# A convolution's output, transposed by DMA instead of by the matrix engine

## The chip, the cores and the metric

The kernel runs on one core of a Trainium2 chip. The core has five engines that each follow their own list of instructions: TensorE (PE, matrix products), VectorE (DVE), ScalarE (ACT), GpSimd (POOL) and SyncE (SP). POOL and SP issue most DMAs. The metric is the device time of one execution in microseconds (us), lower is better.

## What is computed

```python
# x: (8, 4160, 192), weight: (8 heads, 7 taps)
w = softmax(weight, axis=-1)
x_pad = concat([zeros((B, 6, D)), x], axis=1)
# each head owns 24 of the 192 channels; causal convolution over 7 rows
y = einsum('hk,bskhg->bshg', w, unfold(x_pad)).reshape(B, S, D)

# channel mix on y; y_prev is y moved by one row, with a zero row first
xk = mu_k * y + (1 - mu_k) * y_prev
xr = mu_r * y + (1 - mu_r) * y_prev
k  = maximum(xk @ w_k, 0)            # w_k: (192, 1024)
v  = (k * k) @ w_v                   # w_v: (1024, 192)
r  = sigmoid(xr @ w_r)               # w_r: (192, 192)
out = r * v
```

## The kernel before

**Pairs, groups, steps, slots.** The eight sequences are worked on in four pairs. A pair has two sides to its work. The convolution makes its rows in blocks of 116 rows, nine blocks to a group, four groups to a pair (pair 0 splits its first group into five and four blocks). The channel mix takes rows in steps of 512 rows of both sequences, eight steps and a tail of 64 rows. A slot is one of the eight 128-wide pieces of the 1024 hidden units of one step, so a pair has 65 slots, the last of them for the tail, and the whole run 260. Slots are run two at a time ("a pair of slots").

**Convolution.** `load_x` (L70) brings a group of x into `xb` by a casting DMA on POOL's queue, one DMA for each sequence (two for a sequence's first block); `xb` has three buffers. The taps, after the softmax on DVE and ACT (L121 to L130), are written into `w_row`, stored to DRAM (`w_scr`, L137) and read back with a shifted pattern as banded matrices, `toe` (L139). `conv_mm` (L183) is one matmul per head and group, with `toe` as weights; `conv_out` (L197) copies its result from PSUM to `y`, on ACT (in the first group every second one on DVE). `y` has rows on partitions; it has two buffers.

**Transposes.** The mix needs channels on partitions. `tr_mm` (L213) transposes two blocks at a time on PE, three transposes of 128 channels for each block, into PSUM; `tr_out` (L228) copies them on DVE into `yT`, whose three planes are channels 0 to 127 of each sequence, and the last 64 channels of both.

**Mix.** `diff` (L243) subtracts the neighbouring row in `yT`, `mix` (L256) forms `xk` and `xr` on DVE. `k_mm` (L297) makes one slot of k: two matmuls with 128 rows of weights and two with 64, the latter in two halves of the array's rows. `k_relu` (ACT) and `k_square` (DVE) follow. `r_mm`, `r_sig` (ACT), `v_mm` (eight matmuls) and `v_out` (DVE) make the output, two slots at a time, which SP stores from `o_sb` (four buffers).

**Order.** All engines' instructions are issued in the order of a table written out by hand: `at(table, slot, function, ...)` puts a call into a slot for one engine, and the loop at L477 walks the slots from -60. Within a slot POOL's early loads come first, then `k_mm`, then the entries for ACT, PE and DVE. Group g of pair p that is first needed in slot n0 has its conv matmuls in slots c0 to c0 + 7, with c0 = n0 - 22, its transposes from r0 = n0 - 13 on, `diff` in slot n0 - 7 and its x loads in slot c0 - 14. The second and third group of pair 0 are put later (c0 = n0 - 15, r0 = n0 - 7). `r_mm` runs 8 slots behind `k_mm`, `v_mm` 10. PSUM tiles of conv, transposes and r share a pool of two buffers (`psM`).

**The start.** The x load of the first group goes out first, then the weights' loads: `load_w(wk)` (L177) in the program's text, `load_rest` (L168: `wr`, `wv` and zeroed tiles) in slot -16. `nc.scalar.preload_act_table(AF.Sigmoid)` at L147 stands behind the softmax in the text.

Of the kernel before, what the change touches and what calls it, by code (L numbers as in the profile page):

```python
# [7 lines left out]
FP32 = mybir.dt.float32  # L8
BF16 = mybir.dt.bfloat16
AF = mybir.ActivationFunctionType  # L10
# [4 lines left out]
def kernel(  # L15
# [11 lines left out]
    nc = tc.nc  # L27

    B, S, D = x.shape
    H, K = weight.shape  # L30
    G = D // H
    DF = moe_w_k.shape[1]
    P = 128
    NF = DF // P
    LO = D - P
    HALO = K - 1
    BLK = 116
    GB = 9
    NG = 4
    STEP = 512  # L40
    NSTEP = S // STEP
    TAIL = S - NSTEP * STEP
    NPAIR = B // 2
    SPP = NSTEP * NF + 1
    NSLOT = NPAIR * SPP
    YC = 2
    LAG_V = NF + 2
    LAG_R = NF

    const = ctx.enter_context(tc.tile_pool(name="const", bufs=1))  # L50
    two = ctx.enter_context(tc.tile_pool(name="two", bufs=2))
# [4 lines left out]
    psM = ctx.enter_context(tc.tile_pool(name="psM", bufs=2, space=bass.MemoryType.PSUM))  # L56
    dram = ctx.enter_context(tc.tile_pool(name="dram", bufs=1, space=bass.MemoryType.DRAM))


    groups = [  # L60
        [(g * GB, GB, 2 * g) for g in range(NG)]
        if p
        else [(0, 5, 0), (5, 4, 1)] + [(g * GB, GB, 2 * g) for g in range(1, NG)]
        for p in range(NPAIR)
    ]

# [3 lines left out]
    def load_x(p, g):  # L70
        blk0, nb, _ = groups[p][g]
        xb = three.tile([P, GB, 2, D], BF16, tag="xb", name="xb")
        xbs[p, g] = xb
        for s in range(2):
            b = 2 * p + s
            lo, hi = 0, nb
            if blk0 == 0:
                lo = 1
                nc.gpsimd.memset(xb[0:32, 0, s, :], 0.0)
                nc.gpsimd.dma_start(out=xb[HALO:P, 0, s, :], in_=x[b, 0 : P - HALO, :])  # L80
            t0 = blk0 * BLK - HALO
            if b == B - 1 and blk0 + nb == NG * GB:
                hi = nb - 1
                r0 = t0 + hi * BLK
                nc.gpsimd.memset(xb[96:P, hi, s, :], 0.0)
                nc.gpsimd.dma_start(out=xb[0 : S - r0, hi, s, :], in_=x[b, r0:S, :])
            nc.gpsimd.dma_start(  # L87
                out=xb[:, lo:hi, s, :],
                in_=bass.AP(
                    tensor=x.tensor,  # L90
                    offset=x.offset + (b * S + t0 + lo * BLK) * D,
                    ap=[[D, P], [BLK * D, hi - lo], [1, D]],
                ),
            )
# [4 lines left out]
        out=w_raw,  # L99
        in_=bass.AP(tensor=weight.tensor, offset=weight.offset, ap=[[0, P], [K, H], [1, K]]),  # L100
    )
    nc.scalar.preload_act_table(AF.Exp)
    ones_t = const.tile([P, P], BF16)
# [3 lines left out]
    w_row = const.tile([P, H, P], BF16)  # L107
    nc.vector.memset(w_row, 0.0)
    load_x(0, 0)
    ident = const.tile([P, P], BF16)  # L110
    nc.gpsimd.affine_select(
        out=ident,
        in_=ones_t,
# [3 lines left out]
        base=0,  # L117
        channel_multiplier=-1,
    )
    w_max = const.tile([P, H], FP32)  # L120
    nc.vector.tensor_reduce(out=w_max, in_=w_raw, axis=mybir.AxisListType.X, op=ALU.max)  # L121
    w_exp = const.tile([P, H, K], FP32)
    nc.vector.tensor_tensor(
        out=w_exp, in0=w_raw, in1=w_max.unsqueeze(2).to_broadcast([P, H, K]), op=ALU.subtract
    )
    nc.scalar.activation(out=w_exp, in_=w_exp, func=AF.Exp)
    w_sum = const.tile([P, H], FP32)
    nc.vector.tensor_reduce(out=w_sum, in_=w_exp, axis=mybir.AxisListType.X, op=ALU.add)
    nc.vector.reciprocal(out=w_sum, in_=w_sum)
    nc.vector.tensor_tensor(  # L130
        out=w_row[:, :, 0:K],
# [5 lines left out]
    nc.sync.dma_start(out=w_scr, in_=w_row)  # L137
    toe = const.tile([P, H, BLK], BF16)
    nc.sync.dma_start(  # L139
        out=toe,  # L140
        in_=bass.AP(
            tensor=w_scr.tensor,
            offset=w_scr.offset + K - 1,
            ap=[[H * P - 1, P], [P, H], [1, BLK]],
        ),
    )
    nc.scalar.preload_act_table(AF.Sigmoid)  # L147


    mu = const.tile([P, 2, 2], FP32)  # L150
# [12 lines left out]
    def load_w(w, src):  # L163
        nc.gpsimd.dma_start(out=w[:, 0, :], in_=src[0:P, :])
        nc.gpsimd.dma_start(out=w[0:LO, 1, :], in_=src[P:D, :])
        nc.gpsimd.dma_start(out=w[LO:P, 1, :], in_=src[P:D, :])

    def load_rest():  # L168
# [5 lines left out]
        for t in tails:  # L174
            nc.gpsimd.memset(t, 0.0)

    load_w(wk, moe_w_k)  # L177


    ys, yTs = {}, {}  # L180
    conv_ps = {}

    def conv_mm(p, g, h):  # L183
        nb = groups[p][g][1]
        if h == 0:
            ys[p, g] = two.tile([P, GB, 2 * D], BF16, tag="y", name="y")
        ps = psM.tile([P, GB, 2, G], FP32, tag="m", name="ps_c")
        conv_ps[p, g, h] = ps
# [19 lines left out]
            n = c1 - max(c0, P)  # L208
            copy(out=yl[:, :, :, c1 - P - n : c1 - P], in_=ps[:BLK, :nb, :, G - n : G])

    tr_ps = {}

    def tr_mm(p, g, j):  # L213
        blk0, nb, _ = groups[p][g]
        if blk0 == 0 and j == 0:
            yTs[p] = two.tile([P, 3, YC + NG * GB * BLK], BF16, tag="yT", name="yT")
            nc.vector.memset(yTs[p][:, :, 0:YC], 0.0)
        ps = psM.tile([P, 3, 2, BLK], BF16, tag="m", name="ps_t")
        tr_ps[p, g, j] = ps
        for i in range(min(2, nb - 2 * j)):  # L220
            for c in range(3):
                nc.tensor.transpose(  # L222
                    out=ps[:, c, i, :],
                    in_=ys[p, g][:BLK, 2 * j + i, c * P : (c + 1) * P],
                    identity=ident[:BLK, :BLK],
                )

    def tr_out(p, g, j):  # L228
        blk0, nb, _ = groups[p][g]
        ps = tr_ps.pop((p, g, j))  # L230
        n = min(2, nb - 2 * j)
        c0 = YC + (blk0 + 2 * j) * BLK
        nc.vector.tensor_copy(  # L233
# [6 lines left out]
    def step_len(s):  # L240
        return STEP if s < NSTEP else TAIL

    def diff(p, s):  # L243
        L = step_len(s)
        c0 = YC + s * STEP
        d = two.tile([P, 3, STEP], BF16, tag="diff", name="d")
# [9 lines left out]
    def mix(p, s, i, part):  # L256

        L = step_len(s)
        c0 = YC + s * STEP - 1
        d, yT = diffs[p, s], yTs[p]  # L260
# [32 lines left out]
    def where(n):  # L293
        p, r = divmod(n, SPP)
        return p, r // NF, r % NF
# [131 lines left out]
    early, pe, act, dve = ({} for _ in range(4))  # L427

    def at(table, n, fn, *a):
        table.setdefault(n, []).append((fn, a))  # L430

    at(early, -16, load_rest)
    for p in range(NPAIR):
        for g, (blk0, nb, s0) in enumerate(groups[p]):
            n0 = p * SPP + s0 * NF
            late = p == 0 and s0 in (1, 2)
            c0, r0 = (n0 - 15, n0 - 7) if late else (n0 - 22, n0 - 13)
            if n0:
                at(early, c0 - 14, load_x, p, g)
            for h in range(H):  # L440
                at(pe, c0 + h, conv_mm, p, g, h)
                if n0 == 0 and h % 2:
                    at(dve, c0 + 1 + h, conv_out, p, g, h, nc.vector.tensor_copy)
                else:
                    at(act, c0 + 1 + h, conv_out, p, g, h, nc.scalar.copy)
            for j in range((nb + 1) // 2):
                at(pe, r0 + j, tr_mm, p, g, j)
                at(dve, r0 + 1 + j, tr_out, p, g, j)
        for s in range(NSTEP + 1):
            n0 = p * SPP + s * NF  # L450
            late = p == 0 and s in (1, 2)
            at(dve, n0 - (4 if late else 7), diff, p, s)
            for j, (i, part) in enumerate(((0, 0), (0, 1), (1, 0), (1, 1))):
                at(dve, n0 + ((-3, -2, -1, -1)[j] if late else j - 5), mix, p, s, i, part)
    for m in range(NSLOT):
        p, s, t = where(m)
        at(pe, m + LAG_R, r_mm, m)
        last = t % 2 == 1 or s == NSTEP
        if last:
            q = m - t % 2  # L460
            at(act, m + LAG_R + 1, r_sig, q)
            at(dve, m + LAG_V + 1, v_out, q)
        at(pe, m + LAG_V, v_mm, m)

# [4 lines left out]
    def slots():  # L469

        n = -60
        while n < NSLOT + LAG_V + 3:
            two_ = 0 <= n < NSLOT and where(n)[1] < NSTEP
# [48 lines left out]
```

## Time and profile before

| | |
|---|---|
| median of 3 runs | 504.35 us (503.9 to 504.45) |
| profiled execution | 503.97 us, span of its instructions 502.3 us |
| TensorE (PE) busy | 459.3 us, 91% |
| VectorE (DVE) busy | 420.6 us, 84% |
| ScalarE (ACT) busy | 375.6 us, 75% |
| GpSimd (POOL) busy | 45.9 us, 9% |
| DMA | 41.92 MB written by the queues, q0 (POOL) 26.6% and q1 (SP) 17.2% of 16 engines' span |

Busy time is the union of an engine's instructions. PE's matmuls are pipelined, so a matmul's own duration (0.25 us for 192 columns) is longer than the time after which the next one starts; starts are the better measure. "idle before <-X" says what ended an engine's wait. Times in the timeline are from the start of the span.

### The profile page before, as it was taken

The page shows a single profiled execution, that of the slowest core. Times are in us where ns is not written, and L with a number is a line of the kernel's source. Part 1 is how long each engine was busy: PE and PEld are TensorE (multiplying, and loading weights), DVE is VectorE, ACT ScalarE, POOL GpSimd, SP SyncE. Part 2 cuts the span into 40 slices and gives each one's busy share as a digit, 9 for nine tenths or more (in the row PEclk, how much of TensorE's full clock was granted, in tenths as well). Part 3 has the DMA queues.
Part 4 walks back from the last instruction along what each step waited for, and adds up shares of the span by engine and source line. Part 5 has one row for each costly group of instructions (what it writes and reads, how often), then busy time and mean ns, then how long its engine had stood idle before and what let it go on. Part 6 is the DMA issues. An engine that isn't in the chain of part 4 may idle for free.

```text
span 502.3 us, 10506 instructions
## 1 busy us (share of the span) xinstructions
PE 459.3 (91%) x4193; PEld 312.9 (62%) x4256; DVE 420.6 (84%) x676; ACT 375.6 (75%) x545; POOL 45.9 (9%) x69
## 2 busy tenths in 40 slices
PE   0587999999999999999999999999999999999996
PEld 0334666666776666666776666666676666666676
DVE  1487897989889898898899889798998989799872
ACT  3288769687786968778686877868787786967772
POOL 7512100101020010101002010100200000000000
PEclk9999999999999999999999999999999999999999
DMA  9996361826336182722718272351811212112113
GB/s 125 139 141 88 58 117 56 119 64 102 81 65 117 57 120 64 116 67 54 127 49 130 60 117 66 72 110 48 134 48 49 73 48 64 48 55 63 62 62 102
DMA packets 76625, 41.92 MB, mean 83 GB/s; under 512 B 42912, under 2 KB 76192, under 8 KB 76576
## 3 DMA queue, kind: packets, MB, share of 16 engines
q0 software_dynamic: 39184, 15.15, 26.6%
q1 hardware_dynamic: 37392, 26.10, 17.2%
q8 instruction: 33, 0.54, 0.5%
q14 instruction: 16, 0.13, 0.1%
HBM read 30.56 MB, written 25.82 MB: 112 GB/s over the span
## 4 chain that ended last, share of the span: by engine, by line
PE 75%; DVE 12%; issue 5%; ACT 3%; DMA 3%; DVEq 0%; SPq 0%
PE ps_v L399 29%; PE ps_k L311 19%; PE ps_k L318 12%; PE ps_c L189 4%; DVE yT L233 4%; PE ps_r L381 4%; PE ps_r L380 4%; DVE xr L271 3%; PE ps_t L222 3%; DVE k L364 3%; ACT k_sb L350 2%; DMA w_scr<-w_row 1%; DVE xk L271 1%; DVE o_sb L411 1%; DMA w_raw<-in_weight_dram 1%
## 5 line engine op out<-in xcount | busy, mean ns | idle before, releaser
L350 ACT ACTIVATE k_sb<-ps_k 128x1024 bf16<-128x1024 f32 x260 | 260.1, 1025 | 37.0 <-PE ps_k L318 35.1
L399 PE MATMUL ps_v<-wv,k 128*128 128x192 bf16 x2048 | 210.9, 246 | 0.0
L399 PEld LDWEIGHTS <-k 128*128 128x128 bf16 x2048 | 173.0, 98 | 25.8 <-issue 2.8
L364 DVE TENSOR_TENSOR k<-k_sb 128x1024 bf16<-128x1024 bf16 x256 | 175.1, 685 | 13.2 <-ACT k_sb L350 13.1
L311 PE MATMUL ps_k<-xk,wk 128*128 128x512 bf16 x449 | 140.9, 384 | 1.1 <-DVE xk L271 0.3
L389 ACT ACTIVATE r_sb<-ps_r 128x384 bf16<-128x384 f32 x132 | 64.2, 486 | 64.2 <-PE ps_r L381 64.2
L411 DVE TENSOR_TENSOR o_sb<-ps_v,r_sb 128x384 f32<-128x384 f32 x132 | 72.3, 548 | 35.3 <-PE ps_v L399 33.7
L318 PE MATMUL ps_k<-xk,wk 64*128 64x512 bf16 x512 | 78.5, 383 | 8.5 <-ACT k_sb L350 0.9
L311 PEld LDWEIGHTS <-wk 128*128 128x128 bf16 x512 | 37.8, 98 | 56.0 <-issue 55.7
L271 DVE SCALAR_TENSOR_TENSOR xr<-d,mu,yT 128x1024 bf16<-128x1024 bf16 x64 | 64.7, 1015 | 0.9
L271 DVE SCALAR_TENSOR_TENSOR xk<-d,mu,yT 128x1024 bf16<-128x1024 bf16 x64 | 64.8, 1014 | 0.6
L189 PE MATMUL ps_c<-xb,toe 128*116 128x432 bf16 (+2 forms) x136 | 46.5, 348 | 20.3 <-DMA toe<-w_scr 15.8
L380 PE MATMUL ps_r<-wr,xr 128*128 128x192 bf16 x256 | 63.0, 246 | 0.0
L381 PE MATMUL ps_r<-wr,xr 128*128 128x192 bf16 x256 | 63.0, 246 | 0.0
L206 ACT CAST y<-ps_c 116x432 bf16<-116x432 f32 (+4 forms) x99 | 46.3, 468 | 17.9 <-PE ps_c L189 17.4
L87 POOL DMA_DIRECT2D xb<-in_x_dram x34 | 32.1, 949 | 241.0 <-PE ps_c L189 213.3
L318 PEld LDWEIGHTS <-wk 64*128 64x128 bf16 x512 | 15.1, 94 | 56.5 <-issue 56.5
L233 DVE COPY yT<-ps_t 128x696 bf16<-128x696 bf16 (+1 forms) x80 | 38.5, 481 | 9.5 <-PE ps_t L222 8.9
L222 PE MATMUL ps_t<-ident,y 116*128 116x116 bf16 x432 | 36.3, 218 | 8.7 <-DVE yT L233 7.6
L222 PEld LDWEIGHTS <-y 116*128 116x128 bf16 x432 | 29.8, 99 | 21.1 <-issue 11.7
L189 PEld LDWEIGHTS <-toe 128*116 128x116 bf16 x136 | 18.7, 139 | 25.3 <-DMA toe<-w_scr 15.8
L249 DVE TENSOR_TENSOR d<-yT 128x1536 bf16<-128x1536 bf16 (+1 forms) x36 | 31.6, 879 | 0.1
(50 smaller groups left out, 130.2 us busy)
## 6 DMA issues: line engine op xcount, KB each, us to landing
out_dram<-o_sb SPq DMA_DIRECT2D x128, 192.0 KB, 2.0
xb<-in_x_dram POOLq DMA_DIRECT2D x23, 432.0 KB, 7.5
xb<-in_x_dram POOLq DMA_DIRECT2D x7, 384.0 KB, 5.9
xb<-in_x_dram POOLq DMA_DIRECT2D x4, 192.0 KB, 5.8
wv<-in_moe_w_v_dram POOLq DMA_DIRECT2D x1, 384.0 KB, 5.1
out_dram<-o_sb SPq DMA_DIRECT2D x8, 48.0 KB, 2.0
xb<-in_x_dram POOLq DMA_DIRECT2D x8, 45.8 KB, 3.9
wk<-in_moe_w_k_dram POOLq DMA_DIRECT2D x1, 256.0 KB, 5.6
```

What stands on the lines that cost most here:

```text
L189: nc.tensor.matmul(out=ps[:BLK, :nb], lhsT=toe[:, h, :], rhs=xbs[p, g][:, :nb, :, h * G : (h + 1) * G], start=True, stop=True,)
L222: nc.tensor.transpose(out=ps[:, c, i, :], in_=ys[p, g][:BLK, 2 * j + i, c * P : (c + 1) * P], identity=ident[:BLK, :BLK],)
L271: nc.vector.scalar_tensor_tensor(out=o, in0=d[r0:r1, sl, :L], scalar=mu[r0:r1, i, part : part + 1], in1=yT[r0:r1, sl, c0 : c0 + L], op0=AL ...
L311: nc.tensor.matmul(out=ps[:, i, :], lhsT=wk[:, 0, fs], rhs=xk[:, i, :], start=first, stop=not first)
L318: nc.tensor.matmul(out=ps[:, i, :], lhsT=wk[r, 1, fs], rhs=xk[r, 2, :], start=not first, stop=first)
L350: nc.scalar.activation(out=k_sb, in_=ps.rearrange("p a b -> p (a b)"), func=AF.Relu)
L364: nc.vector.tensor_tensor(out=o, in0=k_sb, in1=k_sb, op=ALU.mult)
L380: nc.tensor.matmul(out=o, lhsT=hi, rhs=wr[:, 0, :], start=True, stop=False)
L381: nc.tensor.matmul(out=o, lhsT=lo, rhs=wlo, start=False, stop=True)
L389: nc.scalar.activation(out=r_sb[:, :n, :], in_=ps[:, :n, :], func=AF.Sigmoid)
L399: nc.tensor.matmul(out=o, lhsT=k2[:, f, t * P : (t + 1) * P], rhs=wv[:, f, :], start=(f == 0), stop=(f == NF - 1),)
L411: nc.vector.tensor_tensor(out=o_sb[:, :n, :], in0=v_ps.pop(m)[:, :n, :], in1=r_sbs.pop(m)[:, :n, :], op=ALU.mult)
```

## The change

- Blocks have 112 rows, 38 of them to a pair, in groups of 10, 10, 9 and 9 (pair 0: 5, 5, 10, 9, 9).
- Only the first three groups of pair 0 are still transposed on PE. All other groups write `y` to DRAM (`y_write`, one DMA on SP's queue when the last head's copy is done) and read it back transposed into `yT` (`y_read`, one transposing DMA on SP's queue, five slots later). Their conv matmuls are 8 slots earlier, and so are their x loads. `yT` has 16 columns in front instead of 2.
- 36 dummy matmuls of 512 columns with `w_row` as moving operand, into a tile of `psM`, stand ahead of the softmax.
- A copy of one column of `w_row` on POOL (`gate`) stands ahead of `load_w(wk)`, so that POOL's queue goes on only when the softmax is written.
- A sigmoid of one column of `w_exp` takes the place of the preloading of the sigmoid's table.
- The last block of each sequence, which is only partly filled, is now loaded by a DMA of its own in all pairs, onto a zeroed tile.

```diff
-    BLK = 116
-    GB = 9
-    NG = 4
+    BLK = 112
+    GB = 10
+    NBLK = -(-S // BLK)
...
-    YC = 2
+    YC = 16
     LAG_V = NF + 2
+    WARM = 36
...
     groups = [
-        [(g * GB, GB, 2 * g) for g in range(NG)]
+        [(0, 10, 0), (10, 10, 2), (20, 9, 4), (29, 9, 6)]
         if p
-        else [(0, 5, 0), (5, 4, 1)] + [(g * GB, GB, 2 * g) for g in range(1, NG)]
+        else [(0, 5, 0), (5, 5, 1), (10, 10, 2), (20, 9, 4), (29, 9, 6)]
         for p in range(NPAIR)
     ]
...
-            if b == B - 1 and blk0 + nb == NG * GB:
+            if blk0 + nb == NBLK:
                 hi = nb - 1
                 r0 = t0 + hi * BLK
-                nc.gpsimd.memset(xb[96:P, hi, s, :], 0.0)
+                nc.gpsimd.memset(xb[:, hi, s, :], 0.0)
...
+    warm = psM.tile([P, 4, P], FP32, tag="m", name="warm")
+    for _ in range(WARM):
+        nc.tensor.matmul(
+            out=warm, lhsT=ones_t, rhs=w_row[:, 0:4, :], start=True, stop=True
+        )
     w_max = const.tile([P, H], FP32)
...
     nc.scalar.activation(out=w_exp, in_=w_exp, func=AF.Exp)
+    w_sig = const.tile([P, 1], FP32)
+    nc.scalar.activation(out=w_sig, in_=w_exp[:, 0, 0:1], func=AF.Sigmoid)
...
-    nc.scalar.preload_act_table(AF.Sigmoid)
...
+    gate = const.tile([P, 1], BF16)
+    nc.gpsimd.tensor_copy(out=gate, in_=w_row[:, 0, 0:1])
     load_w(wk, moe_w_k)
...
+    def y_write(p, g):
+        blk0, nb, _ = groups[p][g]
+        if blk0 == 0:
+            new_yT(p)
+        nc.sync.dma_start(
+            out=y_drams[p][blk0 * BLK : (blk0 + nb) * BLK, :].rearrange("(n t) c -> t n c", t=BLK),
+            in_=ys[p, g][:BLK, :nb, :],
+        )
+
+    def y_read(p, g):
+        blk0, nb, _ = groups[p][g]
+        r0, r1 = blk0 * BLK, (blk0 + nb) * BLK
+        nc.sync.dma_start_transpose(
+            out=yTs[p][:, :, YC + r0 : YC + r1], in_=y_drams[p][r0:r1, :]
+        )
...
+            on_pe = p == 0 and s0 < 3
             late = p == 0 and s0 in (1, 2)
             c0, r0 = (n0 - 15, n0 - 7) if late else (n0 - 22, n0 - 13)
+            if not on_pe:
+                c0 -= 8
...
-            for j in range((nb + 1) // 2):
-                at(pe, r0 + j, tr_mm, p, g, j)
-                at(dve, r0 + 1 + j, tr_out, p, g, j)
+            if on_pe:
+                for j in range((nb + 1) // 2):
+                    at(pe, r0 + j, tr_mm, p, g, j)
+                    at(dve, r0 + 1 + j, tr_out, p, g, j)
+            else:
+                at(dve, c0 + H, y_write, p, g)
+                at(dve, c0 + H + 5, y_read, p, g)
```

`new_yT(p)` allocates `yT` and the DRAM tile `y_drams[p]` (rows of 384 channels: both sequences) and zeroes the 16 columns in front.

More of the change, by code (lines that the diff above doesn't have):

```diff
@@ L209, in conv_out, with new_yT @@
             copy(out=yl[:, :, :, c1 - P - n : c1 - P], in_=ps[:BLK, :nb, :, G - n : G])
-    tr_ps = {}
+    tr_ps, y_drams = {}, {}
+    def new_yT(p):
+        yTs[p] = two.tile([P, 3, YC + NBLK * BLK], BF16, tag="yT", name="yT")
+        y_drams[p] = dram.tile([NBLK * BLK, 2 * D], BF16, tag=f"y{p % 2}", name="y_dram")
+        nc.vector.memset(yTs[p][:, :, 0:YC], 0.0)
+    def y_write(p, g):
[12 more added lines that the diff above has]
+        )
     def tr_mm(p, g, j):
@@ L215, in tr_mm @@
         if blk0 == 0 and j == 0:
-            yTs[p] = two.tile([P, 3, YC + NG * GB * BLK], BF16, tag="yT", name="yT")
-            nc.vector.memset(yTs[p][:, :, 0:YC], 0.0)
+            new_yT(p)
         ps = psM.tile([P, 3, 2, BLK], BF16, tag="m", name="ps_t")
```

## The prediction

> **What bounds the kernel now.** I read the page first (busy shares, chain, DMA queues), then the timeline of TensorE in the middle of the run, the busy time by stretches of it, and last the timeline of the first 55 us.
>
> ```profile
> span 502.3 us, 10506 instructions
> PE 459.3 (91%) x4193; PEld 312.9 (62%) x4256; DVE 420.6 (84%) x676; ACT 375.6 (75%) x545; POOL 45.9 (9%) x69
> ...
> q0 software_dynamic: 39184, 15.15, 26.6%
> q1 hardware_dynamic: 37392, 26.10, 17.2%
> ...
> PE 75%; DVE 12%; issue 5%; ACT 3%; DMA 3%; DVEq 0%; SPq 0%
> ...
> out_dram<-o_sb SPq DMA_DIRECT2D x128, 192.0 KB, 2.0
> xb<-in_x_dram POOLq DMA_DIRECT2D x23, 432.0 KB, 7.5
> ...
> w_scr<-w_row SPq DMA_DIRECT2D x1, 256.0 KB, 6.1
> toe<-w_scr SPq DMA_DIRECT2D x1, 232.0 KB, 3.4
> ```
>
> TensorE (PE) is busy for 91% of the span and makes 75% of the chain that ended last; VectorE (DVE) follows with 12%. Because an average mixes stages, I look at one period of 16 slots (one group of conv blocks) and at a stretch near the end that has neither conv nor transposes. Columns: stretch, its length, busy time (and count) of PE, weight load, DVE, ACT and POOL, then PE's granted clock, the DMA engines' busy share and GB/s.
>
> ```profile
> 175.67:204.58 28.91, 27.67 (x257) 18.90 (x260) 25.39 (x39) 22.73 (x34) 1.62 (x3) 1.00 0.46 87
> 453.41:478.66 25.25, 24.66 (x222) 16.57 (x225) 22.50 (x34) 19.44 (x24) 0.00 (x0) 1.00 0.21 64
> 499.00:502.20 3.20, 0.00 (x0) 0.00 (x0) 0.00 (x0) 0.00 (x0) 0.00 (x0) 0.65 0.30 80
> ```
>
> ```profile
> 170.13 0.35 PE L189 MATMUL ps_c<-xb,toe 128*116 128x432 bf16 x1
> 170.31 0.82 PE L399 MATMUL ps_v<-wv,k 128*128 128x192 bf16 x8
> 170.97 0.25 PE L380 MATMUL ps_r<-wr,xr 128*128 128x192 bf16 x1
> ...
> 178.00 0.47 PE L222 MATMUL ps_t<-ident,y 116*128 116x116 bf16 x6
> 178.31 0.83 PE L399 MATMUL ps_v<-wv,k 128*128 128x192 bf16 x8
> ...
> 186.36 0.31 PE L222 MATMUL ps_t<-ident,y 116*128 116x116 bf16 x3 [0.65 <-DVE yT L233]
> ```
>
> Starts, not durations, give the price, since matmuls overlap. A conv matmul takes 0.18 us of PE (170.13 to 170.31), eight v matmuls of 192 columns 0.66 (170.31 to 170.97, so 512 columns go through in about 0.22), six transposes 0.31 (178.00 to 178.31). Both 16-slot stretches hold eight pairs of slots: 25.25 us without conv and transposes, 28.91 with 8 conv matmuls (1.44) and the 27 transposes of one group. So a group's transposes cost 28.91 - 25.25 - 1.44 = 2.22 us: 27 x 0.31/6 = 1.40 of matrix work, and about 0.8 in which PE waits until DVE has emptied a transpose's PSUM tile (the 0.65 in the last row). DVE had 22.50 of 25.25 us busy where no such wait shows, so it keeps up once its copies go. In mid-run, then, PE is the bound and everything taken from it counts.
>
> **The start** is another regime, and the change rearranges it:
>
> ```profile
> 1.14 0.48 DVE L108 MEMSET w_row<- 128x512 uint32 x1
> ...
> 4.67 0.59 POOL L164 DMA_DIRECT2D wk<-in_moe_w_k_dram  x1
> ...
> 5.90 0.22 DVE L130 TENSOR_TENSOR w_row<-w_exp,w_sum 128x56 bf16<-128x56 f32 x1
> ...
> 6.15 0.34 SPq L137 DMA_DIRECT2D w_scr<-w_row  x1
> ...
> 15.78 0.65 PE L189 MATMUL ps_c<-xb,toe 128*116 128x240 bf16 x2 [15.78 <-DMA toe<-w_scr]
> ...
> 17.42 1.99 POOL L87 DMA_DIRECT2D xb<-in_x_dram  x2
> ...
> 19.75 1.96 POOL L87 DMA_DIRECT2D xb<-in_x_dram  x2 [0.35 <-PE ps_c L189]
> ...
> 24.52 1.01 PE L311 MATMUL ps_k<-xk,wk 128*128 128x512 bf16 x2 [0.27 <-DVE xk L271]
> ...
> 28.76 0.69 PE L311 MATMUL ps_k<-xk,wk 128*128 128x512 bf16 x2
> ...
> 31.62 0.59 PE L311 MATMUL ps_k<-xk,wk 128*128 128x512 bf16 x2
> ...
> 32.78 1.05 ACT L350 ACTIVATE k_sb<-ps_k 128x1024 bf16<-128x1024 f32 x1
> ...
> 33.70 0.55 ACT L206 CAST y<-ps_c 116x432 bf16<-116x432 f32 x1
> 34.11 1.06 ACT L350 ACTIVATE k_sb<-ps_k 128x1024 bf16<-128x1024 f32 x1
> ...
> 40.19 0.38 PE L311 MATMUL ps_k<-xk,wk 128*128 128x512 bf16 x1
> ...
> 40.62 1.28 ACT L389 ACT_TABLE_LOAD   x1
> ...
> 51.84 0.38 PE L311 MATMUL ps_k<-xk,wk 128*128 128x512 bf16 x1
> ```
>
> The first conv waits until 15.78 for toe. Slot pairs (0,1), (2,3), (4,5) and (10,11) start at 24.52, 28.76, 31.62 and 40.19. Between 31.62 and 40.19 ScalarE (ACT) sets the pace: relu to conv copy 0.92, copy to relu 0.41, so 1.33 a slot. x is loaded in two halves per group; in the windows 16:19 and 19:22 these landed after
>
> ```profile
> DMA to landing us min/median/max: 6.4/7.0/7.7
> DMA to landing us min/median/max: 7.7/8.7/10.0
> ```
>
> so group 2 (issued 17.42 and about 18.42) was there at 26.1, and group 3 (19.75, about 20.73) at 30.7, 2.3 us for each half of nine blocks. Before the change group 3 is needed in slot 10 only.
>
> **The change part by part.**
>
> 1. Fourteen of the 17 groups lose PE transposes and DVE copies: the last two of pair 0 and all twelve of pairs 1 to 3. 14 x 2.22 = -31.1 us. A group's last copies and waits cannot stay, as nothing issues them.
>
> 2. 38 blocks instead of 36 a pair: a conv matmul has 456 columns on average, not 432. 24 columns at 0.22 per 512 are 0.010 us, times 128 matmuls = +1.3. ACT's copies grow by 5%: 0.41 to 0.43-0.45, on an engine that is 75% busy, hidden in mid-run by PE's slower slots (0.92 + 0.45 + half a sigmoid against 1.76 us of PE a slot); in the start it counts (item 5).
>
> 3. y_write, y_read. A ten-block group is 1120 rows of 768 bytes, 840 KB. The write is like the out stores in form: at least one store (2.0), at most 4.4 stores one after another (8.8); by q1's packets (0.172 x 502.3 x 16 / 37392 = 37 ns each) 1120/16 x 37 = 2.6 plus some 1.5 fixed, about 4. It has five slots, some 8.4 us (half of the 3.34 us that a pair will take, each), before y_read, which waits on it in SP's queue. No transposing DMA is in this trace. From below: x halves land 2.3 us apart, so 4.6 us for two halves of the same bytes; from above, two halves one after another, 15. If each row goes as the three 128-channel pieces of yT, 3360 packets at q0's 54.6 ns (0.266 x 502.3 x 16 / 39184) make 11.5. I take 9, since the bytes are contiguous rows unlike x's strided ones. diff (L249) needs yT ten slots, 16.7 us, after y_read is issued. So I cost the DMAs at nothing; their cover is those ten slots, and each us beyond costs 14 us. Behind y_read in SP's queue stand the out stores. o_sb has four buffers, so a store has four pairs, 13 us, of which it needs 2.0: 11 us of blocking cost nothing. DMA engines have room (shares 0.46 and 0.21 above).
>
> 4. The dummies. They start when w_row is zeroed (1.14 + 0.48) and read w_row; the softmax result goes into the same tile (L130, 5.90), so that write must now wait until the last dummy has read. PE is slow at first: two 512-column matmuls take 1.01 at 24.52 and 0.59 at 31.62, after dense work from 24.52 to 28.76. Nine or so at 0.47, the other 27 at 0.22: 4.2 + 5.9, so the dummies end at about 11.8 (bounds: 36 x 0.22 gives 9.6, 36 x 0.47 gives 18.6) and w_row is ready at 12.1 instead of 6.1. w_scr then has the DMA engines nearly alone: 2.0 (an out store) to 6.1 (as now), I take 2.5 since the weights are behind the gate; toe 3.4 beside the weights' loads, so toe lands at about 18.3, and the first conv is 2.5 us later than now. A gain by PE being warm I set at nothing: conv starts 6.5 us after the last dummy, and in the last row of the stretches the clock is down to a mean of 0.65 within 4.3 us of the last matmul at about 498.
> The Trainium skill, "TensorE: Matmul & The Clock Gate" (Part 1), has a rule that speaks against the dummies: after an idle window of about 3.4 us the clock falls back to half rate. By it the dummies gain nothing, as in my sum; were the clock to hold, pair (0,1) would take the 2.86 of the next pair and not 4.24, and the time would be 1.4 lower. The 0.65 row agrees with the rule.
>
> 5. The gate puts the whole POOL queue behind the softmax: wk, x of group 1, wr, wv, then x of groups 2 and 3. Group 2's issue came 12.75 after wk's (4.67 to 17.42); from a gate at 12.2 it comes at 25.0. Its second half was there 8.7 later (9.2 with ten blocks): 34.2. Group 3's was there 13.3 after that issue, 13.8 now: 38.8. But group 3's conv moves from slot 10 to slot 2, which PE reaches at about 33: pair (2,3) starts 12.98 after the first conv (15.78 to 28.76), so at 31.3 now, and four k matmuls of each of its slots come first. PE stands in order, so pair (4,5) starts near 38.8 + 1.1 = 39.9 instead of 31.62: +8.3. From there ACT has two conv copies a slot for groups 2 and 3: 0.92 + 2 x 0.45 = 1.82 instead of 1.33. Six slots make 10.9 where they took 8.57: +2.3. Slot 10 is 10.6 us late.
>
> 6. Slots 10 to 13 took 51.84 - 40.19 = 11.65. They lose four conv matmuls (0.7) and the sigmoid's table load (1.28), which w_sig moves into idle ACT time before the first conv: -2.0. Four more conv matmuls of group 3 leave slots 14 to 17: -0.7. The transposes of group 2 stay, and with them the rest of the excess over 2 x 3.16.
>
> Sum: -31.1 + 1.3 + 10.6 - 2.0 - 0.7 = -21.9 from the profiled execution's 503.97 (1.67 more than its span; the median is 504.35): 482.
>
> **The rivals.**
>
> A. The start costs nothing: the loads, unmixed with others, land sooner, and ACT's extra is hidden. For it: the DMA engines idle until the gate. Against it: L87's loads are paced by 2.3 us a half, and groups 2 and 3 stand last. Without the 10.6: 471.4.
>
> B. Another wait takes the place of the copies' wait: 0.8 us a group stays because DVE is late for other reasons, or out stores queue behind y_read (from 11 us of blocking on). 14 x 0.8 gives 493; half of the gain gone by stores gives up to 498. For it: the 186.36 row shows DVE close to its limit; against it: 453.41:478.66 runs without a wait.
>
> C. Slower: the transposing read takes longer than its ten slots, and diff waits on DVE's queue in front of the squares. At 18.3 us a group it cancels the gain (21.9/14 = 1.6 beyond 16.7); at 20 us the time is 482 + 14 x 3.3 = 528. For it: no row prices a transpose, and the upper end, 15 us, lies near; if it moved single elements at 37 ns each, 430080/16 x 37 ns would be 1000 us a group. Against it: only 50 GB/s are needed.
> On this the Trainium skill, "DMA: Bandwidth & Descriptors" (Latency and other measured facts), gives 261 GB/s for a transposing DMA, an estimate of 3.3 us a group, by which C could not occur; its rules for kernel authors put an element-wise rearrangement 19 times dearer, by which it would. No run here shows either yet.
>
> D. Nothing changes within 0.2% (about what a measurement here can tell from no change): only if the start and a late read just meet the gain.
>
> **How the numbers follow.** Main course (475 to 490 by the dummies' bounds, -2.2 and +6.8, and the clock's 1.4) 0.62; A 0.12; B 0.12; C 0.12; D 0.02. Faster holds the main course, A and B: 0.86; same 0.02; slower 0.12. The range leaves out C, D and the outer ends of A and B: 470 to 498.
>
> **What would show it.** Right: steady pairs at 3.16 and 3.52 with no 3.77 or 4.43 between them; L130 at about 12; x of group 3 as the wait before conv in slot 2; two conv copies between relus until slot 10; y_read landing below 16 us, with no DVE wait before L249. Wrong: L249 waiting for yT from a DMA in each group; L130 still near 6; v_out waiting for o_sb.

## The result, and the profile after

The changed kernel takes 486.62 us (median; 485.68 to 488.08) against 504.14 of the kernel before in the same runs: a ratio of 0.9655, interval 0.9625 to 0.9684. The forecast was 482, with 470 to 498 as its range. The profiled execution took 485.83 us, with a span of 484.1 instead of 502.3: 18.2 us less, where the sum had 21.9. One execution among all those reported here, the profiled one of the kernel without dummies, took 1149.5 us with PE slow throughout; it is left out of that kernel's time, and no other trace of that kernel was kept.

From the page of the changed kernel:

```profile
span 484.1 us, 9846 instructions
PE 459.3 (95%) x3920; PEld 299.0 (62%) x3920; DVE 390.5 (81%) x607; ACT 374.6 (77%) x544; POOL 51.9 (11%) x84
...
q1 hardware_dynamic: 97200, 48.80, 41.8%
q0 software_dynamic: 40592, 15.62, 28.0%
...
PE 90%; DMA 4%; ACT 2%; POOL 2%; DVE 1%; issue 0%; DVEq 0%; POOLq 0%
```

The chain that ended last is the work that set the end of the run, followed back from its last instruction. DVE's share of it fell from 12% to 1%, and PE's rose from 75% to 90%: behind the start, the waits for DVE's copies are gone. New in the chain are DMA, 4%, and POOL. SP's queue moves nearly twice the bytes.

Busy time by stretches, in the columns of the prediction: 16 slots in mid-run, eight pairs of slots near the end, and a part of the start.

```profile
177.70:204.41 26.71, 26.71 (x234) 17.49 (x233) 23.15 (x34) 22.73 (x33) 1.98 (x2) 1.00 0.77 150
441.83:467.08 25.25, 25.25 (x226) 16.57 (x225) 21.34 (x38) 19.43 (x24) 0.00 (x0) 1.00 0.19 63
16.50:33.50 17.00, 10.34 (x45) 5.17 (x45) 8.50 (x15) 5.73 (x15) 8.24 (x14) 0.50 1.15 137
```

Sixteen slots take 26.71 us where they took 28.91, and PE is busy in all of them: 25.25 for the eight pairs plus eight conv matmuls at 0.18. In the last row PE had half its clock for 17 us of the start. That is no loss against the kernel before, which was as slow there: its first two k matmuls took 1.01 us (24.52), those of the changed kernel 1.01 too (29.43, below), although the profile of the kernel before gives a granted clock of 1.00 for that time.

The DMAs of the changed kernel (name, count, KB, median us to landing; the last line is the spread for the transposing reads):

```profile
y_dram<-y SPq DMA_DIRECT2D x8, 756.0 KB, 7.0
y_dram<-y SPq DMA_DIRECT2D x6, 840.0 KB, 5.5
w_scr<-w_row SPq DMA_DIRECT2D x1, 256.0 KB, 2.0
toe<-w_scr SPq DMA_DIRECT2D x1, 224.0 KB, 6.7
yT<-y_dram SPq DMA_TRANSPOSE x14, 8.9
```

```profile
DMA to landing us min/median/max: 5.4/8.9/12.0
```

A transposing read lands after 8.9 us, where the prediction took 9 between ends of 4.6 and 15, and never later than the 16.7 us that its ten slots give.

The start, from the timeline of the changed kernel:

```profile
1.67 10.17 PE L124 MATMUL warm<-w_row,ones_t 128*128 128x512 bf16 x36 [1.67 <-DVE w_row L109]
...
5.88 0.15 PEld L124 LDWEIGHTS <-ones_t 128*128 128x128 bf16 x1 [0.28 <-issue]
6.28 5.06 PEld L124 LDWEIGHTS <-ones_t 128*128 128x128 bf16 x24 [0.24 <-issue]
...
11.87 0.22 DVE L139 TENSOR_TENSOR w_row<-w_exp,w_sum 128x56 bf16<-128x56 f32 x1 [6.03 <-PE warm L124]
...
14.22 0.40 SPq L148 DMA_DIRECT2D toe<-w_scr  x1
...
20.94 0.65 PE L199 MATMUL ps_c<-xb,toe 128*112 128x240 bf16 x2 [9.11 <-DMA toe<-w_scr]
...
29.43 1.01 PE L343 MATMUL ps_k<-xk,wk 128*128 128x512 bf16 x2
...
36.56 0.41 PE L199 MATMUL ps_c<-xb,toe 128*112 128x480 bf16 x1 [2.98 <-DMA xb<-in_x_dram]
...
41.16 0.39 PE L199 MATMUL ps_c<-xb,toe 128*112 128x432 bf16 x1 [0.61 <-DMA xb<-in_x_dram]
...
46.65 1.04 ACT L216 CAST y<-ps_c 112x480 bf16<-112x480 f32 x2
...
52.82 0.24 PE L412 MATMUL ps_r<-wr,xr 128*128 128x192 bf16 x1 [0.99 <-ACT y L219]
...
54.29 0.34 PE L199 MATMUL ps_c<-xb,toe 128*112 128x432 bf16 x1 [0.60 <-DVE yT L265]
...
54.64 0.59 PE L343 MATMUL ps_k<-xk,wk 128*128 128x512 bf16 x2
...
62.15 0.59 PE L343 MATMUL ps_k<-xk,wk 128*128 128x512 bf16 x2
```

The dummies end at 11.84; the softmax's write had waited 6.03 us for them; the first conv comes at 20.94 instead of 15.78. PE waits for x twice, in slots 1 and 2 (36.56 and 41.16). Copies of conv on ACT come in twos. The pair (10,11) starts at 54.64 instead of 40.19, the pair (14,15) at 62.15 instead of 51.84.

So the 18.2 us are the sum of three stretches:

| stretch | before | after | difference | forecast |
|---|---|---|---|---|
| up to slot 10 | 40.19 | 54.64 | +14.5 | +10.6 |
| slots 10 to 13 | 11.65 | 7.51 | -4.1 | -2.0 |
| from slot 14 on | 450.5 | 421.9 | -28.5 | -30.5 |

### The profile page after: what moved, and what is told of

It reads as the page before. It is cut to its first block, busy times and chain, and to the rows that moved or that the text cites. A ratio compares the mean times of both kernels' runs of the same rounds, so it can differ in the third digit from the quotient of the medians.

```text
span 484.1 us, 9846 instructions
## 1 busy us (share of the span) xinstructions
PE 459.3 (95%) x3920; PEld 299.0 (62%) x3920; DVE 390.5 (81%) x607; ACT 374.6 (77%) x544; POOL 51.9 (11%) x84
## 4 chain that ended last, share of the span: by engine, by line
PE 90%; DMA 4%; ACT 2%; POOL 2%; DVE 1%; issue 0%; DVEq 0%; POOLq 0%
PE ps_v L431 35%; PE ps_k L343 25%; PE ps_k L350 14%; PE ps_c L199 4%; PE ps_r L413 4%; PE ps_r L412 4%; DMA xb<-in_x_dram 3%; PE warm L124 2%; DMA wr<-in_moe_w_r_dram 1%; POOL xb L88 1%; ACT k_sb L382 1%; ACT y L216 1%; ACT y L219 0%; PE ps_t L254 0%; PE ps_k L370 0%; PE ps_k L363 0%
## 5 line engine op out<-in xcount | busy, mean ns | idle before, releaser
L431 PEld LDWEIGHTS <-k 128*128 128x128 bf16 x2048 | 175.2, 98 | 30.3
L343 PE MATMUL ps_k<-xk,wk 128*128 128x512 bf16 x512 | 155.2, 385 | 0.0
L216 ACT CAST y<-ps_c 112x480 bf16<-112x480 f32 (+5 forms) x99 | 47.8, 489 | 23.8 <-PE ps_c L199 19.7
L199 PE MATMUL ps_c<-xb,toe 128*112 128x432 bf16 (+2 forms) x136 | 47.6, 359 | 17.3 <-DMA toe<-w_scr 9.1
L199 PEld LDWEIGHTS <-toe 128*112 128x112 bf16 x136 | 18.4, 136 | 26.5 <-DMA toe<-w_scr 9.6
L219 ACT CAST y<-ps_c 112x432 bf16<-112x432 f32 (+5 forms) x49 | 24.7, 511 | 1.7 <-PE ps_c L199 1.6
L413 PEld LDWEIGHTS <-xr 128*128 128x128 bf16 x256 | 25.0, 98 | 1.3 <-issue 1.2
L412 PEld LDWEIGHTS <-xr 128*128 128x128 bf16 x256 | 25.0, 98 | 0.8 <-issue 0.7
## 6 DMA issues: line engine op xcount, KB each, us to landing
xb<-in_x_dram POOLq DMA_DIRECT2D x14, 432.0 KB, 11.8
```

The lines of the kernel that those rows point to most:

```text
L199: nc.tensor.matmul(out=ps[:BLK, :nb], lhsT=toe[:, h, :], rhs=xbs[p, g][:, :nb, :, h * G : (h + 1) * G], start=True, stop=True,)
L216: copy(out=yh[:, :, :, c0 : c0 + n], in_=ps[:BLK, :nb, :, 0:n])
L343: nc.tensor.matmul(out=ps[:, i, :], lhsT=wk[:, 0, fs], rhs=xk[:, i, :], start=first, stop=not first)
L412: nc.tensor.matmul(out=o, lhsT=hi, rhs=wr[:, 0, :], start=True, stop=False)
L413: nc.tensor.matmul(out=o, lhsT=lo, rhs=wlo, start=False, stop=True)
L431: nc.tensor.matmul(out=o, lhsT=k2[:, f, t * P : (t + 1) * P], rhs=wv[:, f, :], start=(f == 0), stop=(f == NF - 1),)
```

## Experiments

Ratios are against the kernel before in the same runs. The theory at this point: DMA transposes are free because of their ten slots, and all of the loss lies in the start. The rivals: that the transposes' DMAs cost something too, and, within the start, that the dummies, the gate or the rate of the x loads is what costs.

**Without the dummies**

```diff
-    warm = psM.tile([P, 4, P], FP32, tag="m", name="warm")
-    for _ in range(WARM):
-        nc.tensor.matmul(
-            out=warm, lhsT=ones_t, rhs=w_row[:, 0:4, :], start=True, stop=True
-        )
```

> The changed kernel without its 36 dummy matmuls; the gate stays. Theory (the dummies hold up the softmax's write of w_row through the shared tile, and everything behind the gate with it): w_row is written at about 5.9 us instead of 11.87, the first conv starts at about 15 instead of 20.94, the second half of group 2's x is there at about 30.5 instead of 36.5, slot 10 starts at about 48.7 instead of 54.64, and the time falls by 5 to 6 us from 486.6, to about 481. Rival 1 (the dummies pay by a warm PE what they cost): 486 to 488. Rival 2 (the rate of the x loads alone sets the start, whenever they are issued): group 3 is there no earlier than 40 us, time above 485.

480.3 us, ratio 0.9526 (0.9512 to 0.9541). The dummies cost 6 us net, as the theory said, and by the time both rivals fall; the starts that the theory gives for conv and slot 10 could not be read from a trace.

**The dummies on a tile of their own**

```diff
+    w_zero = const.tile([P, 4, P], BF16)
+    nc.vector.memset(w_zero, 0.0)
...
-            out=warm, lhsT=ones_t, rhs=w_row[:, 0:4, :], start=True, stop=True
+            out=warm, lhsT=ones_t, rhs=w_zero, start=True, stop=True
```

> The changed kernel with the dummies reading a zeroed tile of their own instead of w_row, so that the softmax's write waits for nothing. Theory (it is the shared tile, not the dummies, that costs): as without dummies, w_row at about 5.9 and slot 10 at about 48.7; the dummies end at about 11.9, the first conv follows at 14 to 15, and if PE's clock is still full then the start is up to 1.4 us shorter: 479.5 to 481. Rival (the dummies themselves delay something, or do nothing): the same time as without dummies or longer; 486 to 487 if the order on PE and not the tile holds up the start.

480.3 us, 0.9514 (0.9492 to 0.9536): not to be told from no dummies at all, and inside the theory's range. It was the shared tile that cost; the dummies are worth nothing even without it. Two stretches of this kernel's start show why (columns as above):

```profile
12.00:17.00 5.00, 1.79 (x9) 0.92 (x8) 1.17 (x4) 1.07 (x3) 0.38 (x2) 1.00 1.15 141
17.50:34.00 16.50, 12.93 (x55) 5.52 (x55) 9.25 (x15) 6.81 (x15) 8.89 (x13) 0.50 1.38 160
```

The clock is full when the first conv starts (at 14.67; its first two matmuls take 0.41 us, against 0.65 in the changed kernel). But PE is busy for only 1.79 of these 5 us, with a wait of 2.34 for toe among them, and the clock falls for the next 17 us, the first k matmuls included. The Trainium skill, "TensorE: Matmul & The Clock Gate" (Part 1), says that an idle window takes the clock back to half. The changed kernel agrees (PE idle from 11.84 to 20.94, half the clock from 16.5); here a stretch with a third of PE's time in use was enough.

**Without dummies and without the gate**

```diff
-    gate = const.tile([P, 1], BF16)
-    nc.gpsimd.tensor_copy(out=gate, in_=w_row[:, 0, 0:1])
```
(and no dummies)

> The changed kernel without dummies and without the gate: the start's loads go out as in the kernel before, only the transposes by DMA, the block sizes and the early sigmoid table stay. Theory (the gate delays the x loads by the softmax's 1.6 us and more, and does not speed toe enough to make up for it): the first conv at about 15.8, group 2 there at about 26.6 and group 3 at about 31.3, hardly a wait on x in slots 1 and 2, slot 10 at about 45 to 46.5, time 476.6 to 478. Rival (the gate clears the way for toe, which is what the start hangs on): the first conv later than with the gate and without the dummies, and a time over 481.

478.19 us, 0.9481 (0.9463 to 0.9498), just above the theory's 476.6 to 478. From its DMAs and its timeline:

```profile
w_scr<-w_row SPq DMA_DIRECT2D x1, 256.0 KB, 6.6
toe<-w_scr SPq DMA_DIRECT2D x1, 224.0 KB, 3.8
```

```profile
16.50 0.65 PE L192 MATMUL ps_c<-xb,toe 128*112 128x240 bf16 x2 [16.50 <-DMA toe<-w_scr]
...
45.83 0.59 PE L336 MATMUL ps_k<-xk,wk 128*128 128x512 bf16 x2
```

Without the gate w_scr takes 6.6 us instead of 2.0, but toe 3.8 instead of 6.7: the gate moves the collision from the store to the read that follows. Slot 10 starts at 45.83, as forecast for this kernel (45 to 46.5), and the gate as it stands costs 2 us (480.3 to 478.19). The rival was right that the gate brings the first conv forward (14.67 in the kernel with the dummies on their own tile, which has the gate, against 16.50 here). But there PE then waits 2.14 us for x in slot 1, and here it waits for no x.

**The start alone, on the kernel before**

```diff
     LAG_V = NF + 2
+    WARM = 36
...
+    warm = psM.tile([P, 4, P], FP32, tag="m", name="warm")
+    for _ in range(WARM):
+        nc.tensor.matmul(
+            out=warm, lhsT=ones_t, rhs=w_row[:, 0:4, :], start=True, stop=True
+        )
...
+    w_sig = const.tile([P, 1], FP32)
+    nc.scalar.activation(out=w_sig, in_=w_exp[:, 0, 0:1], func=AF.Sigmoid)
...
-    nc.scalar.preload_act_table(AF.Sigmoid)
...
+    gate = const.tile([P, 1], BF16)
+    nc.gpsimd.tensor_copy(out=gate, in_=w_row[:, 0, 0:1])
```

> The kernel before with the change's start alone: 36 dummies on w_row, the gate and the early sigmoid table, with transposes on PE, blocks of 116 and groups as before. Theory: the first conv at about 20.9 instead of 15.78, the second half of group 2 there at about 36 so that PE waits for it about 2.5 us in slot 1, group 3 not needed before slot 10, 1.3 us back from the table: 504.1 + 5.2 + 2.5 - 1.3 = 510.5, that is, slower by 6. Rival (the dummies and the gate are worth their place): 502 to 504.

508.32 us, 1.0078 (1.0063 to 1.0094): slower by 4.1 us. The theory had the sign and 6. PE waits for x only once, for 0.18 us, and the stretch of ACT's two copies does not occur, because group 3 is still needed in slot 10:

```profile
21.14 0.66 PE L198 MATMUL ps_c<-xb,toe 128*116 128x240 bf16 x2 [9.35 <-DMA toe<-w_scr]
33.97 0.39 PE L198 MATMUL ps_c<-xb,toe 128*116 128x432 bf16 x1 [0.18 <-DMA xb<-in_x_dram]
...
45.53 0.59 PE L320 MATMUL ps_k<-xk,wk 128*128 128x512 bf16 x2
```

Slot 10 starts at 45.53, 5.3 us later than in the kernel before: so much the dummies and the gate cost by themselves. What the transposes' DMA needs, group 3 early, costs about 5.6 by itself (45.83, in the kernel without dummies and gate). Together they cost 14.5, some 3.5 more than the sum: x comes late where conv needs it early.

**The transposing read eight slots later**

```diff
-                at(dve, c0 + H + 5, y_read, p, g)
+                at(dve, c0 + H + 13, y_read, p, g)
```

> The changed kernel with y_read eight slots later, so that two slots (3.3 us) and not ten lie between its issue and the subtraction that needs it. Theory (the read takes its 5.4 to 12.0 us, median 8.9, and is free only because of the ten slots): VectorE waits a median of 5.6 us in front of the subtraction in each of the 14 groups; if the squares' two slots of lead over the v matmuls absorb some 3 us of that, 14 x 2.6 = 36 us are lost, 523 us; if nothing absorbs it, 14 x 5.6 = 78, 565 us. Rival (the read is hidden anyway, or a wait of VectorE costs nothing while TensorE is the bound): 485 to 490.

489.44 us, 0.9716 (0.9678 to 0.9755), some 3 us more than the changed kernel, whose interval it just touches. Neither the theory nor its milder form holds; the time is inside the rival's 485 to 490. From its waits and the spread of its reads:

```profile
DVE d L281 <- DMA yT<-y_dram: 31.1, 14, 4.1
```

```profile
DMA to landing us min/median/max: 5.2/5.6/7.6
```

DVE does wait in front of the subtraction, in all 14 groups, 31.1 us together. But the read, issued after the x loads have passed, lands in 5.6 us and not 8.9, so a wait is 2.2 us on average and not 5.6. And PE loses little by them. By the starts of its pairs of slots, 13 of the 14 waits, up to 3.9 us long, cost it nothing. Only behind the longest, 4.1 us, does PE fall back: slots 62 to 64, a pair and the tail, take 7.1 us instead of 4.9, and v matmuls wait there until DVE has emptied their PSUM:

```profile
150.61 0.82 PE L431 MATMUL ps_v<-wv,k 128*128 128x192 bf16 x8 [1.69 <-DVE o_sb L443]
```

Another 1.6 us of this trace is not the read's: PE had half its clock from 54.8 to 58.2, in slots 10 and 11, before the first of these waits. The cover of a late yT is thus ten slots and some 4 us of DVE's lead beyond them. How much more it would bear was not tried.

**Two buffers for the output tile**

```diff
-        o_sb = four.tile([P, 2, D], FP32, tag="o_sb", name="o_sb")
+        o_sb = two.tile([P, 2, D], FP32, tag="o_sb", name="o_sb")
```

> The changed kernel with two buffers for o_sb instead of four. Theory (while SyncE is busy issuing a transposing read for 5.4 to 8.3 us, the out stores stand behind it, and four buffers are what makes that free): with two buffers a store has two pairs of slots, 6.5 us, in which it must be issued and land, so VectorE's output product waits in each of the 14 groups for 2 to 5 us, 510 to 550 us, with waits of o_sb on a store's DMA in the trace. Rival (the stores get through beside the read, or the wait is absorbed): 485 to 490.

490.69 us, 0.974 (0.9717 to 0.9763): 4 us more than the changed kernel. The mechanism is there, its price a fraction of the expected:

```profile
DVE o_sb L443 <- DMA out_dram<-o_sb: 35.8, 22, 4.1
```

DVE waits 35.8 us for stores, in 22 places. By the starts of its pairs of slots PE loses time at four of them, 0.6 to 1.8 us each and 5.0 together; 1.6 more in this trace are half a clock in slots 10 and 11, as in the kernel above. What keeps SP busy is the issue of the transposing reads, for 3.4 to 10.0 us each and not 5.4 to 8.3. In the changed kernel, the durations of all 14 (least, median, most in ns, first and last start), and one in the timeline, with three stores right behind it:

```profile
L241 SPq DMA_TRANSPOSE yT<-y_dram x14: 3395/6477/10022, 65.2 to 418.4; - x14
```

```profile
65.22 8.33 SPq L241 DMA_TRANSPOSE yT<-y_dram  x1
73.66 1.59 SPq L448 DMA_DIRECT2D out_dram<-o_sb  x3
```

**The fourth group of pair 0 later (no dummies, no gate)**

```diff
-                c0 -= 8
+                c0 -= 5 if n0 == 4 * NF else 8
```

> The changed kernel without dummies and gate, and with the fourth group of pair 0 (first needed in slot 32) put 5 slots earlier than in the kernel before instead of 8: its conv runs in slots 5 to 12 and not 2 to 9, its read has seven slots. Theory (the two conv copies of a slot on ScalarE set the pace between slots 3 and 9): three slots fewer with two copies, 3 x 0.5, and no wait for x in slot 2, up to 1.0: 475.7 to 477 against 478.2 without this edit. Rival (the pace there is set by something else, or the later read comes late): 478 to 480.

476.37 us, 0.9459 (0.9439 to 0.9479), inside the theory's range and 1.8 us below the kernel without this edit (1.1 by the ratios, whose intervals overlap). Pairs (4,5) and (10,11) of this kernel start here:

```profile
32.41 0.59 PE L336 MATMUL ps_k<-xk,wk 128*128 128x512 bf16 x2
...
43.60 0.59 PE L336 MATMUL ps_k<-xk,wk 128*128 128x512 bf16 x2
```

Slots 4 to 9 take 11.2 us instead of 12.1 (33.72 to 45.83 without this edit), and what is ahead of them is 1.3 shorter too; not by a wait for x, as the theory had it, for without the edit PE did not wait for x there. Of these 2.2 us slots 10 to 13 give back 1.3: they take 8.8 instead of 7.5, with three of the conv matmuls back in them.

**And the weights of r and v behind the x of the third group**

```diff
-    at(early, -16, load_rest)
+    at(early, -11, load_rest)
```

> As the one before, and with the loads of the weights of r and v five slots later in GpSimd's queue, behind the x of the third group. Theory (the third group's x waits in that queue behind a wait for wr): that x is there at about 20 us instead of 27, so that PE does not wait for it in slot 1; 1 us less than the one before, 474.7 to 476. Rival (PE does not wait for x there in any case): the same within 0.5 us; or the v weights come late for slot 10: more than the one before.

480.31 us, 0.9528 (0.9514 to 0.9542): 4 us more, and for a reason that neither side had named. The third group's x is there at 22.2 instead of 28.0, as the theory wanted, but:

```profile
toe<-w_scr SPq DMA_DIRECT2D x1, 224.0 KB, 8.0
```

With x in flight instead of POOL's wait for wr, toe takes 8.0 us; it is there at 21.2 instead of 16.8, and the whole start moves with it. The wait for wr, in the way as it seemed, had kept x's loads out of toe's way.

**A gate on toe, x ahead of the weights of r and v**

```diff
+    gate = const.tile([P, 1], BF16)
+    nc.gpsimd.tensor_copy(out=gate, in_=toe[:, 0, 0:1])
     load_w(wk, moe_w_k)
...
-    at(early, -16, load_rest)
+    at(early, -8, load_rest)
```

> As the kernel with the fourth group put later (no dummies, no gate; 476.4), with a gate that waits until toe has landed, and with the loads of the weights of r and v behind the x of the third and fourth groups. Theory (toe is a DMA of many small pieces that lands late only because other loads are in flight: 3.4 to 8.0 us so far, against 2.0 for w_scr alone): toe is issued at about 8.3 and lands by 11.5, the first conv is 5 us earlier than 16.9; wk (issued 11.2) is there at 15 and group 2 at about 24, about when slot 1 needs it; slot 10 starts 3 to 5 us earlier than 43.6, time 471.5 to 473.5. Rival (the 16 DMA engines' total of loads sets the start, in whatever order): group 2 comes late by as much as toe comes early, 475.5 to 478.

475.62 us, 0.942 (0.94 to 0.9441). From its DMAs, its waits and its timeline:

```profile
w_scr<-w_row SPq DMA_DIRECT2D x1, 256.0 KB, 2.1
toe<-w_scr SPq DMA_DIRECT2D x1, 224.0 KB, 2.8
```

```profile
PE ps_c L194 <- DMA toe<-w_scr: 11.2, 1, 11.2
```

```profile
19.94 0.65 PE L194 MATMUL ps_c<-xb,toe 128*112 128x240 bf16 x2 [2.99 <-DMA xb<-in_x_dram]
```

Alone, toe takes 2.8 us and conv starts at 11.19, the 5 us earlier that the theory asked for. But the time stays within 1 us of the kernel with the fourth group later, as the rival said: PE now waits for x of the second group, and slot 10 comes 2 us earlier, not 3 to 5. Of these 2 us this trace loses 1.4 again to half a clock from 41.3 to 44.6. The spread of the five executions goes with the clock: the two with a mean of 0.999 and 1.0 took 473.6 and 473.8 us, the three with 0.996 took 475.6 to 475.9.

**The same gate, the weights of r and v in their old place**

```diff
-    at(early, -8, load_rest)
+    at(early, -16, load_rest)
```

> As the one before, with the loads of the weights of r and v in their old place, ahead of the x of the third and fourth groups. Theory: toe by 11.5 as well, but group 2's x is issued 13 us after the gate, at about 24, and is there at about 33, some 9 us after slot 1 could use it; slot 10 later than 43.6 by 4 to 6 us, time 480 to 483. Rival (only toe counts): the same time as the one before within 1 us.

483.23 us, 0.9587 (0.9574 to 0.96), just above the theory's 480 to 483. toe lands in 2.7 us here too, and the run is 7.6 us longer all the same:

```profile
PE ps_c L194 <- DMA xb<-in_x_dram: 10.6, 2, 7.5
```

The last two kernels differ in the order of loads alone: what an early toe gains is lost when x does not follow it at once.

The fastest kernels, the one with the fourth group later and the one with the gate on toe, are 5.4% to 5.8% below the kernel before, and 10 to 11 us below the change as made; their intervals overlap, so which of the two is faster is open.

## Why the prediction was right, step by step

**Transposes (step 1)**: right in kind. The period that it took lost 2.20 us (28.91 to 26.71), where 2.22 less 0.08 for the larger conv matmuls was forecast. PE is busy in all of the 26.71, so no wait for DVE is left; the split into 1.4 of matrix work and 0.8 of waiting is not confirmed by that, for PE's idle time fell by 1.24. From slot 14 on 28.5 us are gone and not 30.5, because the step took one period for all. The 16 slots right behind it gained less, before and after:

```profile
204.58:233.32 28.74, 27.50 (x257) 18.77 (x259) 25.39 (x39) 22.33 (x33) 1.95 (x2) 1.00 0.47 87
204.41:231.33 26.92, 26.92 (x235) 17.53 (x233) 23.15 (x35) 23.01 (x33) 3.39 (x6) 1.00 0.72 144
```

These are 1.82 us. By the starts of the pairs of slots, the four periods of each of pairs 1 and 2 gain 1.95, 2.2, 1.8 and 1.8 us; the prediction had taken the largest.

**The DMAs (step 3)**: nothing paid, as said: no instruction of DVE waits for yT's DMA in the changed kernel. The read took 8.9 us where 9 was taken. The write takes 5.5 to 7.0 and not 4; the first one, beside four x loads, took 10, so SP waited for it a little beyond its five slots. The step was right that ten slots cover it, but the price that it put on lateness, 14 us for each us beyond the slots, was wrong: with two slots left, 31.1 us of waiting cost PE 2.2. The rival in which the read comes late was therefore further off than 18 us a group, and the one in which stores queue behind it costs 4 us even with half the buffers. The Trainium skill, "DMA: Bandwidth & Descriptors" (Latency and other measured facts), has 261 GB/s for transposing DMAs (with a non-contiguous middle dimension); 840 KB would take 3.3 us by it, an estimate. The shortest landing of such a read in any run here took 5.1 us. But an out store of 192 KB, a quarter of the bytes, took 2.0, so a landing does not go by the bytes alone, and 5.1 neither bears the rate out nor refutes it. Beside the x loads the median was 8.9. The conclusion, that the late read could not occur, stands.

**The dummies (step 4)**: the mechanism is there, and the end to the tenth of a microsecond: 11.84 (11.8), with the write of w_row behind it (6.03 us of wait). The spacing of their weight loads, 0.43 until about 6 and then 24 in 5.06, fits a clock that doubles there; the granted clock is given as 1.00 all along and does not show it. The prediction set the dummies' gain at nothing; the kernel with the separate tile shows that to be so. The term that was mis-sized is toe: 3.4 was carried over, 6.7 measured, so the first conv came 5.2 and not 2.5 us later. The step argued that w_scr would run nearly alone, which it did (2.0), and set toe beside the weights' loads at the old price. But with a fast w_scr toe is issued 1.9 us after wk's first load (14.22 to 12.29) and not 7.7 (12.35 to 4.67 before), in the midst of these loads and the second group's x. The miss cost little by itself, since PE waited 2.98 us for x later on.

**The gate and group 3 (step 5)**: PE's two waits for x in slots 1 and 2, and then two copies a slot, are there. x of group 3 was forecast for 38.8, and conv needing it ran at 41.16: 2.4 us of the miss. The four halves were issued as forecast (from 25.25 on, forecast 25.0) and landed some 2.3 to 2.6 us apart, but the first took 8.7 us to land and not 6.4; why was not settled. Slots 4 to 9 took 12.1 instead of 10.9. Their pace was the forecast one, 1.8 us a slot, up to slot 8; the 1.2 are the pair (8,9), in which PE waits 0.99 for a conv copy on ACT and 0.60 for a copy of transposes on DVE (52.82 and 54.29). Together the start is 3.9 us longer than said. The clock fell once more behind the wait at 36.56, to half for 3.4 us, but PE still had to wait for x after it (41.16), so it set nothing there.

**Slots 10 to 13 (step 6)**: the gain was twice what was booked, 4.1 us, and this is the step whose reasoning failed. They had an excess over PE's own work that was attributed to the transposes of group 2, which stay; it went when group 3's conv left these slots. The kernel with the start alone separates the two terms: with the table load moved and conv still there the slots take 10.7 us instead of 11.65 (45.53 to 56.21), so the table was worth 1.0 (1.28 booked), and conv's leaving 3.2 (0.7 booked). In the kernel before, conv's matmuls stood in these slots until DVE had copied transposes out of the PSUM buffers that both share:

```profile
44.86 0.34 PE L189 MATMUL ps_c<-xb,toe 128*116 128x432 bf16 x1 [0.61 <-DVE yT L233]
...
50.62 0.34 PE L189 MATMUL ps_c<-xb,toe 128*116 128x432 bf16 x1 [1.62 <-DVE yT L233]
```

Both waits are there in the kernel with the start alone too; with the 0.7 of the matmuls they make 2.9 of the 3.2.

The misses are +3.9 in the start, -2.1 in slots 10 to 13 and +2.0 from slot 14 on. That the second takes away part of the other two is luck, and the time lies as near to 482 as it does by that. The rival in which the start costs nothing would have given 471.4; the starts as mended in the experiments came to 475.6 at best.

## What to carry to other kernels

Ask of each warm-up or filler instruction which tile it reads: a read of a tile that the critical path writes later is a wait on that path, and here it cost 6 us for no gain. A chain of small DMAs at the start lives or dies by what else is in flight, so what has to be ordered is the whole list of loads, not one of them. Moving work from a full engine to DMA needs its slack paid somewhere; here it was paid in the start, where an earlier conv met loads that were not there yet. And a price read from one period of a repeating kernel holds for that period: compare the others before multiplying it.

## What the runs showed of the hardware that had not been expected

- Issuing one transposing read kept SP's queue busy for 3.4 to 10.0 us, where a plain DMA took 0.40 (toe's read); stores behind it are issued when it is done.
- A 224 KB read in short pieces took 2.8 us alone and 3.8 to 8.0 us beside loads.
- PE's clock, once lowered, stayed at half for 17 us of the start although PE was busy for 12.93 of 16.50 us in one kernel and 10.34 of 17.00 in another; in the kernel with the later read it stayed so from 17.3 to 44.5, with PE busy for 19.23 of 27.20 us.
- The granted clock of a profile can read 1.00 at the start while matmuls run at half speed: in the kernel before two of 512 columns took 1.01 us at 24.52 and 0.59 at 31.62, with 1.00 given for both.
